# A kernel's opening stage: scratch laid out by half, fewer and larger reloads, the second input's loads and two sums moved

## The chip, the cores and the metric

The kernel runs on one core of one Trainium2 chip. The figure of merit is the device time of one execution in microseconds (us), the median over several runs. A core has five engines that run their own instruction streams and wait for each other through semaphores: TensorE (PE, matrix products; PEld is its loading of weights), VectorE (DVE), ScalarE (ACT), GpSimd (POOL) and SyncE (SP, which here only issues DMAs). ACT and POOL issue DMAs too.

## The reference, cut to what matters

```python
X = np.fft.rfft(x, axis=1)                     # x: 8 x 3008 x 256, float32
Y = X * (filt_r + 1j * filt_i)[None]           # 1505 frequencies x 256 channels
y = np.fft.irfft(Y, n=3008, axis=1).astype(np.float32)
h = y.reshape(24064, 256) @ w_in               # 256 x 2048
g = h * (1.0 / (1.0 + np.exp(-h)))             # SiLU
out = (g @ w_out).astype(np.float32)           # 2048 x 256
```

The two weight matrices arrive as 64-bit floats, the rest as 32-bit floats.

## The kernel before

**The main loop.** The length 3008 is 47 x 64, and each transform is done as matrix products with small tables. The two large products use a scheme with seven block products in place of eight (names A11, A12, S1 to S4, A22), on 2 x 2 blocks of the weights. Work is cut into 384 *steps*: 8 batches, 2 halves of a batch, 3 column ranges, 8 slices `jp` of the hidden width. A step is seven products into the hidden layer (`hidden`, L734, with the SiLU and sums on ACT and DVE) and, one step later, seven out of it (`project`, L797). Step s uses slice s mod 8, so slices 2 and 3 of the weights are first needed in steps 2 and 3. What else there is to do (the spectral stages of the next batch, weights not yet unpacked) is put into the steps as pieces with a step number and a round of eight (`put`), so that it runs beside them.

**The ramp.** Before step 0 batch 0 has to pass through the spectral stages alone, and the weights of the first slices have to be unpacked. This change lies in the ramp's end and in the first two steps. The ramp is written out by hand from L997 to L1111; each engine takes its instructions in that order. Its stages for batch 0 are:

- `stage1_first` (L299): the 47-point part, from x loaded into the room that the weights `w_t` will take later; DVE transposes it into a view `t2`, also within `w_t`.
- For each of six groups g: `forward` (L446), `multiply` by the filter (DVE, L468), `inverse_first` (L511), then `rows_first` (L518, L521), which copies two PSUM banks to SBUF and stores them to a DRAM scratch `d2`. Group g's two stores fill rows 8g to 8g+7 of `d2`.
- `load_t4` (L546) reads `d2` back with other axes on the partitions: rows 0 to 47 of one half h on 48 partitions, four values of n for a piece. It is called for four pieces and three row ranges (0 to 24, 24 to 32, 32 to 48), each time for both halves: 24 DMAs, all on SP but the second half's last four, which are on ACT.
- `stage3` (L562) for pieces 0 to 3, the last 47-point products, and the copies of their results into `y` (L576, or L244 and L246 by turns on DVE and ACT). Step 0 needs all four.

In `d2[row, n, half, channel]` both halves of a row lie side by side for each n, so one half's run of contiguous bytes is 256 channels, 1 KB.

**Fillers.** While PE has nothing to do it multiplies tables into a spare bank (`idle`, 128 columns, L1009; `idle_wide`, 256 columns, L1015; and the `fill` of `stage3`, L554). They compute nothing that is used.

**Weights in the ramp.** `split` (L922, L925 on DVE; L924, L926 and, for some slices, L931, L932 on ACT), `rounded` (L938, L940, L944 on DVE) and `placed` (L953) turn the 64-bit words of slice j into 32-bit floats in `w_t`. `combine_weights(jp)` (L705) forms four sums of 128 x 256 for a pair of slices: pairs 1, 2 and 3 on GpSimd, pair 0 on DVE.

**Batch 1.** `second` is batch 1's part. Its `stage1` (L333, two products of 512 columns, and L349, two copies on ACT) sits in steps 0 to 7; `load_x(0)` and `weights(9)` are issued on SP in the middle of the ramp (L1081, L1082).

**Banks.** In the ramp `bank` hands out the eight PSUM banks in turn by the counter `early`; after the ramp batch 1's stage 1 uses the two banks of tag `f`.

## Time and profile before

| | |
|---|---|
| median of 3 runs | 2583.8 us (2583.6 to 2589.22) |
| the profiled execution, its own time | 2582.95 us |
| its span, first to last instruction | 2581.1 us |
| mean granted TensorE clock | 0.998 |
| PE busy in the span | 2560.4 us (99%) |
| DVE, ACT, POOL busy | 1679.8, 1112.5, 424.0 us |
| the ramp: start of step 0's first product | 80.25 us from the span's start |

The times of lines are microseconds from the start of the span. "Busy" of PE is modelled, since matmuls are pipelined, so 99% busy doesn't say that PE is at its peak; it includes the fillers. One product in the program is two records of PE in the trace: "x42" under L1015 are 21 products. A row of the timeline gives start, length, engine, line, operation, result and operands, count, and in brackets how long the engine was idle before it and what ended that.

### The profile page before, as it was taken

The numbers are of one execution on the slowest core, as the hardware profiler recorded it, in microseconds if no ns is written. First come the engines' busy times: TensorE is split into PE (matmuls) and PEld (weight loads), VectorE is DVE, ScalarE is ACT, GpSimd is POOL, SyncE is SP. The second block draws the span as 40 slices with busy tenths as digits, with TensorE's granted clock in tenths as the row PEclk, the third lists the DMA queues.
The fourth block names the chain that finished last, engine by engine and source line by source line (L and its number), as shares of the span: only waits on it lengthen the run. The fifth ranks groups of instructions, "written<-read, shape, count | busy, mean of one in ns | idle before, by whom it ended". The sixth has DMA issues, their size and how long they took to land.

```text
span 2581.1 us, 48332 instructions
## 1 busy us (share of the span) xinstructions
PE 2560.4 (99%) x18956; PEld 2197.1 (85%) x18956; DVE 1679.8 (65%) x3569; ACT 1112.5 (43%) x3014; POOL 424.0 (16%) x672
## 2 busy tenths in 40 slices
PE   8999999999999999999999999999999999999998
PEld 6788888888888888888888888888888888888987
DVE  7866666666666666666666666666666666555554
ACT  3544444444444444444444444444444444444443
POOL 2211111121112111311122111211121112101101
PEclk9999999999999999999999999999999999999999
DMA  8531232222222222322223122331232211200000
GB/s 279 156 74 49 72 79 63 60 63 75 60 63 69 70 62 58 77 72 66 61 65 83 50 66 58 80 80 46 66 85 64 69 42 33 58 19 16 9 17 17
DMA packets 200077, 171.08 MB, mean 66 GB/s; under 512 B 122116, under 2 KB 174196, under 8 KB 199060
## 3 DMA queue, kind: packets, MB, share of 16 engines
q1 hardware_dynamic: 178520, 117.04, 18.5%
q0 software_dynamic: 16928, 44.65, 5.4%
q10 hardware_dynamic: 4400, 6.29, 0.8%
q8 instruction: 149, 2.44, 0.4%
q14 instruction: 80, 0.66, 0.1%
HBM read 96.05 MB, written 81.26 MB: 69 GB/s over the span
## 4 chain that ended last, share of the span: by engine, by line
PE 96%; DVE 1%; DMA 1%; ACT 1%; issue 0%; ACTq 0%; POOL 0%; SPq 0%; DVEq 0%; POOLq 0%
PE acc L797 43%; PE px L734 25%; PE pyz L734 19%; PE pd L562 3%; PE pb L446 2%; PE pc L489 2%; PE pf L416 1%; DMA filt<-in_filt_r_dram 1%; DVE g L705 0%; DMA w_t<-in_x_dram 0%; PE pa L342 0%; PE pc L511 0%; PE idle L1015 0%; ACT t L349 0%; ACTq L233 0%
## 5 line engine op out<-in xcount | busy, mean ns | idle before, releaser
L797 PE MATMUL acc<-g,w_t 128*128 128x256 f32 (+1 forms) x5376 | 1509.1, 375 | 0.4 <-DVE g L705 0.4
L797 PEld LDWEIGHTS acc<-g,w_t 128*128 128x128 f32 x5376 | 1021.8, 190 | 115.2 <-DVE g L705 0.8
L705 DVE TENSOR_TENSOR g<-pyz,abc 128x256 f32<-128x256 f32 (+1 forms) x1152 | 479.3, 416 | 613.4 <-ACT abc L755 359.6
L705 DVE TENSOR_TENSOR g<-g 128x256 f32<-128x256 f32 (+3 forms) x1152 | 598.2, 519 | 196.5 <-ACT g L738 183.4
L734 PE MATMUL px<-ty,w_t 128*128 128x256 f32 (+1 forms) x2304 | 677.9, 376 | 0.7 <-ACT abc L755 0.6
L738 ACT ACTIVATE g<-g 128x256 f32<-128x256 f32 (+1 forms) x1152 | 472.9, 410 | 250.0 <-DVE g L705 250.0
L734 PEld LDWEIGHTS px<-ty,w_t 128*128 128x128 f32 x2304 | 432.3, 190 | 64.4 <-issue 7.9
L705 POOL TENSOR_TENSOR s<-s 128x256 f32<-128x256 f32 (+1 forms) x329 | 254.7, 791 | 1412.9 <-DVE s L817 1307.8
L734 PE MATMUL pyz<-y,w_t 128*128 128x256 f32 (+1 forms) x1536 | 453.8, 377 | 0.0
L734 PEld LDWEIGHTS pyz<-y,w_t 128*128 128x128 f32 x1536 | 283.2, 189 | 48.1 <-DVE g L705 8.9
L749 ACT COPY abc<-px 128x256 f32<-128x256 f32 (+1 forms) x384 | 141.1, 368 | 365.2 <-PE px L734 365.2
L755 ACT COPY abc<-px 128x256 f32<-128x256 f32 (+1 forms) x384 | 141.6, 369 | 336.3 <-PE px L734 335.6
L738 ACT ACTIVATE g<-px 128x256 f32<-128x256 f32 (+1 forms) x384 | 145.8, 380 | 297.6 <-PE px L734 297.5
L734 PE MATMUL px<-y,w_t 128*128 128x256 f32 (+1 forms) x768 | 231.9, 384 | 0.1
L734 PE MATMUL pyz<-ty,w_t 128*128 128x256 f32 (+1 forms) x768 | 225.3, 375 | 0.2 <-DVE g L705 0.2
L734 PEld LDWEIGHTS px<-y,w_t 128*128 128x128 f32 x768 | 140.0, 189 | 33.2 <-DVE y L584 5.8
L734 PEld LDWEIGHTS pyz<-ty,w_t 128*128 128x128 f32 x768 | 144.3, 190 | 18.8 <-DVE g L705 1.0
L742 ACT COPY abc<-px 128x256 f32<-128x256 f32 (+1 forms) x384 | 135.4, 353 | 43.7 <-PE px L734 43.7
L562 PEld LDWEIGHTS pd<-wi_t,t 48*64 48x64 f32 x4096 | 65.7, 135 | 28.8 <-ACT g L738 16.4
L428 POOL DMA_DIRECT2D d<-tf x144 | 71.4, 503 | 29.5 <-DVE tf L424 25.4
L817 ACT COPY s<-acc 128x512 f32<-128x512 f32 (+1 forms) x94 | 54.2, 577 | 47.6 <-PE acc L797 47.5
L562 PE MATMUL pd<-wi_t,t 48*64 48x47 f32 x4096 | 72.2, 233 | 2.5 <-issue 2.2
(124 smaller groups left out, 1316.0 us busy)
## 6 DMA issues: line engine op xcount, KB each, us to landing
t<-d SPq DMA_DIRECT2D x120, 192.0 KB
d<-q POOLq DMA_DIRECT2D x86, 256.0 KB, 2.6
t<-d SPq DMA_DIRECT2D x84, 256.0 KB
out_dram<-o SPq DMA_DIRECT2D x636, 32.0 KB
d<-tf POOLq DMA_DIRECT2D x144, 96.0 KB, 3.2
xr<-in_x_dram SPq DMA_DIRECT2D x6, 1472.0 KB
x_all<-in_x_dram SPq DMA_DIRECT2D x72, 96.0 KB
x_all<-xr SPq DMA_DIRECT2D x72, 96.0 KB
```

The costliest lines, as they stand in the source:

```text
L428: nc.gpsimd.dma_start(out=d1[k // 2, :, k % 2, n0:n0 + 4], in_=us["tf"][32 * k:32 * k + NS].rearrange("p q n c -> p (q n) c"))
L446: nc.tensor.matmul(out=ps[k][32 * j:32 * j + 32, ri, :], lhsT=d_t[rows, 4 * g + at, ri, :], rhs=t2[rows, at, :], start=True, stop=True)
L489: nc.tensor.matmul(out=ps[j][64 * k:64 * k + 64, a, :], lhsT=e_t[rows, g + a, k, ri, :], rhs=zs[k][rows, ri, :], start=(a == 0 and ri == 0 ...
L562: nc.tensor.matmul(out=ps[h][c0:c0 + 64, cb, i, :], lhsT=t4s[g][rows, i, 128 * cb + c0:128 * cb + c0 + 64], rhs=wi_t[rows, :], start=True, ...
L705: eng.tensor_tensor(out=out, in0=in0, in1=in1, op=op)
L734: nc.tensor.matmul(out=out, lhsT=w_t[:, jp, c, 0], rhs=rhs, start=start, stop=True, skip_group_check=True)
L738: nc.scalar.activation(out=g[:, k, 0:n], in_=g[:, k, 0:n] if src is None else src, func=AFT.Silu)
L742: nc.scalar.copy(out=sums[:, 0, 0:n], in_=xo)
L749: nc.scalar.copy(out=sums[:, 1, 0:n], in_=xo)
L755: nc.scalar.copy(out=sums[:, 2, 0:n], in_=xo)
L797: nc.tensor.matmul(out=acc[pair][i][:, h, 0:n], lhsT=w_t[:, jp, c, 1], rhs=g[:, k, 0:n], start=(jp == 0 and h == 0), stop=last, skip_group ...
L817: copy(out=s[:, 2 * i:2 * i + 2, 0:n], in_=acc[pair][i][:, :, 0:n])
```

## The change

It touches the ramp from group 3 on, and three things in the first steps.

- The scratch of batch 0 becomes `d2[half, row, n, channel]`. The reload of the first 16 n is one row range and one half per DMA (`load_t4_rows`): 6 DMAs, all on SP, each moving 16 KB contiguous per row, in place of 24 with 1 KB pieces. They land in a view `t4` within `w_t` (the room of `t2`, slots that `forward` of groups 2 to 5 reads) instead of four tiles of two pools. The stores write 1 KB pieces instead of 2 KB.
- The first reload (rows 0 to 24) is issued after `forward(5)`; rows 24 to 32 come after group 4's stores in program order, rows 32 to 48 after group 5's.
- Batch 1's `load_x(0)` and `weights(9)` are issued behind all six reloads.
- Group 4's stores go out from ACT instead of GpSimd. Group 5 copies into tiles of pool `z`, its second copy on DVE instead of ACT, and its copies stand behind `rounded(4, 5)`.
- `combine_weights(2)` leaves GpSimd and the ramp; its halves run on DVE at the ends of steps 0 and 1. `combine_weights(3)` stays on GpSimd behind a one-column copy (`gate`) that waits for `placed(8)`.
- Slice 4's last exponent operation goes from two ACT instructions (L931, L932) to one DVE instruction (L940).
- Fillers: 12 wide and 12 narrow products in place of 21 wide ones; the two wide fills in `stage3` of pieces 1 and 2 go. After pieces 1 and 2 batch 1's first two stage 1 products are done (`rows_product`); they leave step 0.
- Copies into `y`: pieces 0 and 1 all on ACT, pieces 2 and 3 one on ACT and one on DVE (before, by turns).
- The bank counter is set so that `stage3` leaves the two `f` banks to `rows_product`.

```diff
-        d2 = dpool.tile([2 * NS, 32, 2, C], FP32, name=f"d2_{b}", tag="d2")
+        d2 = dpool.tile([2 * NS, 32, 2, C] if b else [2, 2 * NS, 32, C], FP32, name=f"d2_{b}", tag="d2")
...
+            us["t4"] = view[:, 8960:13056].rearrange("p (n c) -> p n c", c=C)
...
+        def rows_product(u, h, ps=None):
+            if ps is None:
+                ps = bank(b, f"pa_{b}_{u}_{h}")
+                us.setdefault("rows", []).append(ps)
+            nc.tensor.matmul(out=ps.rearrange("p n c -> p (n c)"), lhsT=wx_t,
+                             rhs=xs[u][0:96, 512 * h:512 * h + 512], start=True, stop=True)
...
         def rows_first(g):
             for i, pool, tag in ((0, qpool, "q"), (1, opool, "o")):
+                if g == NG - 1:
+                    pool, tag = zpool, "z"
                 qt = pool.tile([128, 2, C], FP32, name=f"q_{b}_{g}_{i}", tag=tag)
-                nc.scalar.copy(out=qt, in_=halves[g][i])
+                copy = nc.vector.tensor_copy if g == NG - 1 and i == 1 else nc.scalar.copy
+                copy(out=qt, in_=halves[g][i])
                 a0 = 8 * g + 4 * i
-                queue = nc.gpsimd if g == NG - 2 else nc.scalar
-                queue.dma_start(out=d2[a0:a0 + 4].rearrange("a n h c -> (a n) h c"), in_=qt)
+                nc.scalar.dma_start(out=d2[:, a0:a0 + 4].rearrange("h a n c -> (a n) h c"), in_=qt)
...
+        def load_t4_rows(first, last):
+            for h in range(2):
+                nc.sync.dma_start(out=us["t4"][64 * h + first:64 * h + last], in_=d2[h, first:last, 0:16, :])
...
-                if g == 0:
-                    nc.scalar.copy(out=dst[:, :, h, n0:n0 + 4], in_=ps[h])
-                else:
-                    evac(dst[:, :, h, n0:n0 + 4], ps[h])
+                copy = nc.vector.tensor_copy if g > 1 and h == 1 else nc.scalar.copy
+                copy(out=dst[:, :, h, n0:n0 + 4], in_=ps[h])
...
-            if j in (0, 2, 4, 6):
+            if j in (0, 2, 6):
...
             part["rows_first"](2)
-            for later in range(4):
-                part["load_t4"](later, 0, 24)
-            second["load_x"](0)
-            weights(9)
+        if g == 3:
+            part["load_t4_rows"](0, 24)
...
     part["rows_first"](3)
-    for later in range(4):
-        part["load_t4"](later, 24, 32)
     split(4, 5)
     combine_weights(0)
-    for g in (4, 5):
-        part["rows_first"](g)
+    part["rows_first"](4)
+    part["load_t4_rows"](24, 32)
     rounded(4, 5)
+    part["rows_first"](5)
+    part["load_t4_rows"](32, 2 * NS)
+    second["load_x"](0)
+    weights(9)
     placed(4, 5)
     split(6, 7, 8)
-    combine_weights(2, eng=gp)
-    for g in range(4):
-        part["load_t4"](g, 32, 2 * NS)
     rounded(6, 7)
     placed(6, 7)
-    combine_weights(3, eng=gp)
     rounded(8)
     placed(8)
-    idle_wide(21)
+    gp.tensor_copy(out=gate, in_=w_t[:, 4, A11, 0, 0:1])
+    combine_weights(3, eng=gp)
+    stand = bank(0, "stand")
+    idle_wide(12, stand)
+    idle(12, stand)
     last_x = x_t[1].rearrange("p a n -> p (a n)")[0:96, 0:256]
     for g in range(4):
-        part["stage3"](g, fill=((), (wide_rows,), (wide_rows,), (last_x,))[g])
+        early[0] = 1 if g in (0, 3) else early[0]
+        part["stage3"](g, fill=(last_x,) if g == 3 else ())
+        if g in (1, 2):
+            second["rows_product"](0, g - 1)
     idle_wide(2)
...
+    for k in range(2):
+        put(k, 7, combine_weights, 2, k)
```

More of the change, by code (lines that the diff above doesn't have):

```diff
@@ L221 @@
     warm = cpool.tile([128, 1], FP32)
+    gate = cpool.tile([128, 1], FP32)
     bias_t = cpool.tile([128, 5], FP32)
@@ L236, in load_filters @@
                                     ap=[[94 * C, 16], [t * C, last - first], [1, C]]))
-    flip, early = [0], [0]
-    def evac(dst, src):
-        flip[0] ^= 1
-        if flip[0]:
-            nc.vector.tensor_copy(out=dst, in_=src)
-        else:
-            nc.scalar.copy(out=dst, in_=src)
+    early = [0]
     y = {}
@@ L325, in sums @@
             us[u] = ut
+        def rows_product(u, h, ps=None):
[4 more added lines that the diff above has]
+                             rhs=xs[u][0:96, 512 * h:512 * h + 512], start=True, stop=True)
         def stage1(u):
             t1 = tpool.tile([128, 2, 2, C], FP32, name=f"t1_{b}_{u}", tag="t")
-            ps = [bank(b, f"pa_{b}_{u}_{h}", HIDDEN[h] if b > 1 and u == 6 else None) for h in range(2)]
+            ps = None
+            if b > 1 or u > 0:
+                ps = [bank(b, f"pa_{b}_{u}_{h}", HIDDEN[h] if b > 1 and u == 6 else None) for h in range(2)]
             if b == 1:
-                xt = xs.pop(u)
-                for h in range(2):
-                    nc.tensor.matmul(out=ps[h].rearrange("p n c -> p (n c)"), lhsT=wx_t,
-                                     rhs=xt[0:96, 512 * h:512 * h + 512], start=True, stop=True)
+                if u > 0:
+                    for h in range(2):
+                        rows_product(u, h, ps[h])
+                else:
+                    ps = us["rows"]
+                xs.pop(u)
                 if u + 2 < 8:
@@ L537, in rows, with load_t4 @@
                 nc.gpsimd.dma_start(out=d2[a0:a0 + 4].rearrange("a n h c -> (a n) h c"), in_=qt[:, a])
-        def load_t4(g, first=0, last=2 * NS):
-            if first == 0 and b == 0 and g in (2, 3):
-                t4s[g] = tpool.tile([128, 4, C], FP32, name=f"t4_{b}_{g}", tag="t")
-            elif first == 0:
-                t4s[g] = t4pool.tile([128, 4, C], FP32, name=f"t4_{b}_{g}", tag="t4")
-            for h in range(2):
-                queue = nc.scalar if first == 32 and h == 1 else nc.sync
-                queue.dma_start(out=t4s[g][64 * h + first:64 * h + last],
-                                in_=d2[first:last, 4 * g:4 * g + 4, h, :])
+        def load_t4(g):
+            t4s[g] = t4pool.tile([128, 4, C], FP32, name=f"t4_{b}_{g}", tag="t4")
+            for h in range(2):
+                rows = d2[:, 4 * g:4 * g + 4, h, :] if b else d2[h, :, 4 * g:4 * g + 4, :]
+                nc.sync.dma_start(out=t4s[g][64 * h:64 * h + 2 * NS], in_=rows)
+        def load_t4_rows(first, last):
+            for h in range(2):
+                nc.sync.dma_start(out=us["t4"][64 * h + first:64 * h + last], in_=d2[h, first:last, 0:16, :])
         def stage3(g, home=None, fill=()):
@@ L556, in stage3 @@
                   .rearrange("p (a i n) -> p a i n", a=2, i=4) for t in room]
+            t4 = us["t4"][:, 4 * g:4 * g + 4] if b == 0 and g < 4 else t4s[g]
             for cb in range(2):
@@ L563, in stage3 @@
                                 out=ps[h][c0:c0 + 64, cb, i, :],
-                                lhsT=t4s[g][rows, i, 128 * cb + c0:128 * cb + c0 + 64],
+                                lhsT=t4[rows, i, 128 * cb + c0:128 * cb + c0 + 64],
                                 rhs=wi_t[rows, :], start=True, stop=True)
@@ L574, in stage3 @@
             for h in range(2):
-                if g == 0:
-                    nc.scalar.copy(out=dst[:, :, h, n0:n0 + 4], in_=ps[h])
-                else:
-                    evac(dst[:, :, h, n0:n0 + 4], ps[h])
+                copy = nc.vector.tensor_copy if g > 1 and h == 1 else nc.scalar.copy
+                copy(out=dst[:, :, h, n0:n0 + 4], in_=ps[h])
         def evict_y(g, h):
@@ L584, in evict_y @@
             copy(out=dst[:, :, h, n0:n0 + 4], in_=us["pd", g][h])
-        return dict(evict_y=evict_y, evict_t1=evict_t1, halves=halves, load_first=load_first, stage1_first=stage1_first, load_x=load_x, sums=sums, stage1=stage1, reverse_x=reverse_x,
+        return dict(evict_y=evict_y, evict_t1=evict_t1, halves=halves, load_first=load_first, stage1_first=stage1_first, load_x=load_x, rows_product=rows_product, sums=sums, stage1=stage1, reverse_x=reverse_x,
                     load_fold=load_fold, fold=fold, stage1_fold=stage1_fold, evict_fold=evict_fold,
-                    load_t2=load_t2, forward=forward, multiply=multiply, add=add, inverse=inverse, inverse_first=inverse_first, rows_first=rows_first, even=even, rows=rows, load_t4=load_t4, stage3=stage3)
+                    load_t2=load_t2, forward=forward, multiply=multiply, add=add, inverse=inverse, inverse_first=inverse_first, rows_first=rows_first, even=even, rows=rows, load_t4=load_t4, load_t4_rows=load_t4_rows, stage3=stage3)
     pending = []
@@ L938, in round_weights @@
             v.scalar_tensor_tensor(out=mf, in0=lo, scalar=2.0 ** -52, in1=mf, op0=ALU.mult, op1=ALU.add)
-            if j not in (0, 2, 4, 6):
+            if j not in (0, 2, 6):
                 v.tensor_scalar(out=e, in0=ef, scalar1=255.0, scalar2=float(1 << 23),
```

## The prediction

> **What bounds the kernel now.** I read the page first:

> ```profile
> span 2581.1 us, 48332 instructions
> PE 2560.4 (99%) x18956; PEld 2197.1 (85%) x18956; DVE 1679.8 (65%) x3569; ACT 1112.5 (43%) x3014; POOL 424.0 (16%) x672
> PE 96%; DVE 1%; DMA 1%; ACT 1%; issue 0%; ACTq 0%; POOL 0%; SPq 0%; DVEq 0%; POOLq 0%
> ```

> The whole is bound by PE; 2450 us of it, from about 130 us on, is not touched. So the change can move the time only by when PE leaves the ramp and how it gets through the first steps. For that I read the chain that ended last, up to 140 us (start, length, what):

> ```profile
> 51.67 10.52 PE pc L511 x192
> 62.19 9.26 PE idle L1015 x42
> 71.70 1.21 issue
> 72.90 1.14 PE pd L562 x62
> ...
> 79.35 0.82 ACT y L246
> ...
> 95.93 0.33 DVE g L705
> 96.53 0.76 DVE g L705 x2
> ...
> 128.92 0.35 DVE g L705
> 129.31 0.70 PE pyz L734 x2
> ```

> Two readings. First, between the inverse products (over at 62.19) and `stage3` PE does 9.26 us of fillers, then stands 1.21 us, although the fillers are over: the data of `stage3` is late, at 72.9. Second, from step 0 to 129 us the chain runs through DVE and ACT, not PE: there a step takes about 7.85 us (DVE e of L922 in the chain at 97.66, 105.51, 113.47, 121.32), while PE's 14 products of 0.43 and two of 0.86 make 7.74. PE is all but full, yet DVE sets the pace.

> Why the data is late shows in the timeline, engine by engine (rows of SP, ACT, POOL, then DVE):

> ```profile
> 57.67 0.72 SPq L906 DMA_DIRECT2D raw<-in_moe_w_out_dram  x1
> 62.95 6.58 SPq L546 DMA_DIRECT2D t<-d  x12
> ...
> 62.84 0.33 ACTq L521 DMA_DIRECT2D d<-q  x1
> 63.88 0.33 ACTq L521 DMA_DIRECT2D d<-q  x1
> 69.44 1.88 ACTq L546 DMA_DIRECT2D t<-d  x4
> ...
> 63.62 3.45 POOL L705 TENSOR_TENSOR w_t<-w_t 128x256 f32<-128x256 f32 x4 [0.47 <-DVE w_t L953]
> ...
> 63.45 0.42 DVE L922 TENSOR_SCALAR scratch<-raw 128x512 uint32<-128x512 uint32 x1
> 63.79 0.95 DVE L925 TENSOR_SCALAR scratch<-raw 128x512 uint32<-128x512 uint32 x1
> 88.53 0.42 DVE L705 TENSOR_TENSOR g<-pyz,abc 128x256 f32<-128x256 f32 x1
> ```

> SP waits from 58.4 to 62.95 for group 3's stores, which were issued at 55.94 and 56.93 and by the trace's completion records land at 61.1 and 62.9, among the loads of x and slice 9; then it needs 6.58 us for 12 issues. The last store (63.88) lands at 67.7. The last four reloads stand on ACT behind `split(6, 7, 8)`, to 69.44; the first of them lands at 72.8, which is when `stage3` starts. `split` itself runs slow, 0.95 for 0.42 us, while GpSimd does its four sums.

> [...] the completion of an 8-row reload moves once some 0.1 us after its issue and then eight times as data lands, that of a 16-row reload sixteen times as data lands. [...] PE idle 3.06 us to 32.48, mean clock 0.91 from 20 to 40 us; the 1.21 us stand costs nothing (1.00).

> **The change, part by part.** All times are before's.

> *The reloads.* Group 4 and 5: products end at 62.19. ACT needs no L931 and L932 for slice 4 (0.71 and 0.72), so group 4's copies and stores go at 59.7 to 61.2. Group 5's first copy is 0.58 and its issue 0.33: 62.2 to 63.15. Its second is on DVE, behind `rounded(4, 5)`: without ACT's L931 and L932, but with one more L940 (0.42), this still ends at 62.07, so the copy runs 62.25 to 62.95 (a 128x512 DVE operation from PSUM is 0.68) and ACT issues its store at 63.2 to 63.5. Landing: 2.5 us from issue (the store at 50.52 lands at 53.0), so 65.7. SP then issues two reloads, 0.43 each. The 16-row reload of 67.83 landed 2.2 us after its issue with 4 KB for each engine; now it is 16 KB, for which the trace's nearest packet (12 KB in 0.46) gives 0.61. First half 68.4, second 69. Rows 0 to 24 go at 53.1 on 12 engines, two rows of 0.61 each and half, done by 58; rows 24 to 32 wait for group 3's stores, which now have no loads of x and weights among them (59.5). Both are hidden. So data is there at **69.0**, against 72.8.

> *The fillers.* 12 wide at 9.26/21 = 0.441 are 5.29. A narrow one: eight at L1009 from 47.78 to 49.76, 0.2475 each, 12 are 2.97. PE reaches `stage3` at 62.19 + 8.26 = **70.45**; this, not the data, is now last, with 1.4 us to spare. Against 72.90: −2.45.

> *Within `stage3`.* Before, 6.29 us (72.90 to 79.19): four pieces and three fills of 0.63 (73.97 to 74.60). After: two fills less, −1.26; two products of 512 columns, 0.86 and the same 0.19 for changing over, +2.10. +0.84. x for them is issued at 66.6, behind the reloads, and needs some 3.6 us: there by 70.2, wanted at 72.7; hidden. ACT has six copies of 0.75 to 0.86 from 71.6 on and PE is longer, so no bank is late. Then 1.06 to step 0 as before (the last copy). Step 0's start: 80.25 − 2.45 + 0.84 = **78.64**, −1.61.

> *Step 0.* The two products it loses were 1.72 of PE; but the chain there is y, ty, g, e (DVE), e, m (ACT), and the two copies L349. None moves. PE waits instead: 0. If PE were the limit it would be −1.7.

> *The sums of pair 2.* Off GpSimd: DVE's `split` gets back about 4 x 0.53 = 2.1, which is hidden (`placed(8)` ends about 73.8 instead of 76.5; step 0 is later). On DVE: a dependent pair 0.34 + 0.43 = 0.77 at step 0's end (as 109.46 in the chain) and an independent one, 0.67, at step 1's. Queued behind each are g's next sum, then `split(10)` or `split(11)`, then ACT. DVE's slack there is 0.12 before 88.53 (its previous operation ends at 88.41) and none at 96.53. So +0.65 + 0.67 = **+1.32**, and since the chain stays with DVE to 129, it isn't won back. Bounds: 0 if PE, which is nearly as full, would have made DVE wait anyway; 1.44 with no slack.

> *Nothing else.* The gated sums of pair 3 run on GpSimd from 73.8, 2.9 to 3.9 us, and are wanted in step 3; DVE's copies of y read PSUM. Nothing on SP is behind anything later than before. Piece 4 and 5's reloads get 4 KB runs; hidden.

> Sum: −2.45 + 0.84 + 1.32 = **−0.3 us** on the profiled 2582.95 (span 2581.1 and 1.85 around it). The median of the runs is 0.85 above that execution: 2583.8 − 0.3 = **2583.5**.

> **The rivals.**
> - *The sums on DVE are hidden.* For: PE's records in steps 1 to 6 leave no gap of theirs, so DVE's lead may be a tie. Against: the chain. −1.6: 2582.2.
> - *Slower: the reloads are late.* One mechanism: stores and reloads in series behind group 5, with all of `stage3` behind one wait in place of four pieces that each waited for its own. For: before needed 9 us from store to use. Against: 1.4 us to spare. Decides from 70.45 on, each us costs one; at 73 it is +2.3 (2586). PE would be cold after about 3 us of standing, +1.7. To leave 0.3% the data would have to come at about 77.
> - *PE goes cold in step 0.* Without the two products its PE has about 2.6 us of gaps, but in pieces of 0.3 to 1.2, shorter than the stand at 71.70 that cost nothing. If it did: up to +1.7 for 3.4 us at half clock, 2585.
> - *The shifted work isn't on the path at all*, so that step 0 starts as before: then only +1.3, 2585.

> **How the numbers follow.** Forecast 0.42, sums hidden 0.25, late reloads 0.13, cold PE or no gain 0.12, and something that I haven't seen 0.08. 0.3% is 7.75 us, about what a measurement of this kernel can tell from no change; none of the named cases reaches it, so same takes all but a late reload gone far wrong or the unseen: 0.90 same, 0.06 slower, 0.04 faster. The range takes in the hidden sums with shorter fillers (−2.7, 2581) and late reloads (2587), and a us for the spread of the runs.

> **What would show it.** Right: fillers from 62.2 to 70.4 with no stand after them; 6 reloads on SP, the last issued near 66; step 0 at 78.6; the DVE operations after 86 offset by −1.6, after 96 by −0.3; PE from 130 us on the same. Wrong: an "issue" piece before L570 in the chain (late data), a clock under 1.00 between 70 and 90, or step 0 at 80 or later.

## The result, and the profile after

The changed kernel takes 2595.71 us in the median of four runs (2593.55 to 2596.37), against 2583.95 us (2583.6 to 2589.22) for the kernel before on the same chip. The ratio is 1.0039, with a 95% interval of 1.0022 to 1.0057; here and below ratios are worked out from the single executions, so they aren't the quotient of the medians (1.0046). It is slower by some 12 us, where a gain of 0.3 was forecast, and outside the predicted range of 2580 to 2588. The ratio lies beyond the 0.3% (7.75 us) that was taken as the bound, but its interval reaches below that. The profiled execution took 2595.21 us, its span is 2593.4 us, and the mean granted clock of TensorE is 0.995 (0.993 to 0.995 in the four executions) where before had 0.998.

From the page of the kernel after, the span, the busy times and the shares of the chain that ended last:

```profile
span 2593.4 us, 48308 instructions
PE 2568.1 (99%) x18958; PEld 2201.3 (85%) x18958; DVE 1678.5 (65%) x3574; ACT 1112.4 (43%) x3012; POOL 419.1 (16%) x667
PE 96%; DMA 1%; DVE 1%; ACT 1%; issue 1%; SPq 0%; ACTq 0%; DVEq 0%
```

PE is busy for 7.7 us more with two records more: a count of busy time can't say where the 12 us lie. The chain can. Kernel after, the chain that ended last in order of time (start, length, what):

```profile
51.85 10.52 PE pc L516 x192
62.37 5.38 PE stand L1021 x24
67.75 2.69 PE stand L1015 x24
70.44 3.61 issue
74.33 1.53 issue
75.86 3.66 PE pd L570 x126
79.52 2.00 PE pa L325 x2
...
90.16 0.85 PE px L740 x2
...
141.74 0.70 PE pyz L740 x2
```

The fillers end at 70.44, as forecast. Then PE stands 5.1 us (two pieces of "issue", with two small products at 74.05 between them) before `stage3` can begin in earnest at 75.86. In `stage3` each thing takes 1.6 to 1.9 times as long as at full clock: two pieces, 126 records of L570, 3.66 us, where before took 1.14 for 62; a product of 512 columns, two records, 2.00 (2.08 in the timeline) where e1_fill below has 1.12 in its timeline. Step 0 starts at 89.95 (before 80.25). The last line answers to before's 129.31: +12.43. After that nothing more is added.

Kernel after, a row of the timeline of SP and one of ACT, and from SP's waits between 36 and 92 us the first (us waited, times, longest):

```profile
53.31 16.94 SPq L554 DMA_DIRECT2D w_t<-d  x6
```

```profile
63.02 0.89 ACTq L528 DMA_DIRECT2D d<-q  x2
```

```profile
SPq L554 <- DMA d<-q: 22.3, 6, 7.1
```

Group 5's stores are issued at 63.02 and 63.48, as forecast. But the six reloads spread over 16.94 us, and what SP waits for, before every one of them, is a store. In the trace's completion records the stores of group 5 land at 68.84 and 69.42, not at 65.7; the last two reloads go at 69.48 and 69.85 and land at 73.84 and 75.77.

The third reading is the clock. Kernel after, busy times of each engine in stretches of the ramp's end (columns: the stretch and its length, then PE, PEld, DVE, ACT and POOL with their instructions, granted clock, DMA share, GB/s):

```profile
72.00:76.00 4.00, 0.42 (x8) 0.36 (x11) 2.32 (x5) 0.00 (x0) 1.81 (x4) 0.86 0.75 122
76.00:90.00 14.00, 14.00 (x265) 10.18 (x266) 2.40 (x4) 4.44 (x6) 1.28 (x2) 0.50 0.32 85
```

From 74.86 to 91.93 us, for 17.07 us, TensorE runs at half clock, and again from 95.34 to 98.76 (3.41). All of `stage3` lies in it, with PE busy for 14.00 of 14 us. By the chain some 7.4 us of it are the small products of L570, the rest wider ones.

So the difference up to step 3's first product, at 115.03 against 102.61, splits like this:

| stretch | before, us | after, us | difference |
|---|---|---|---|
| start of `stage3`, from the span's start | 72.90 | 75.86 | +2.96 |
| `stage3` to step 0 | 7.35 | 14.09 | +6.74 |
| step 0 to step 1 | 6.64 | 7.79 | +1.15 |
| step 1 to step 2 | 7.83 | 8.64 | +0.81 |
| step 2 to step 3 | 7.89 | 8.65 | +0.76 |
| sum | | | +12.42 |

The profiled times differ by 2595.21 − 2582.95 = 12.26.

### The profile page after: what moved, and what is told of

Same layout as the page of the kernel before. It is cut to its first block, busy times and chain, and to the rows that moved or that the text cites. A ratio compares the mean times of both kernels' runs of the same rounds, so it can differ in the third digit from the quotient of the medians.

```text
span 2593.4 us, 48308 instructions
## 1 busy us (share of the span) xinstructions
PE 2568.1 (99%) x18958; PEld 2201.3 (85%) x18958; DVE 1678.5 (65%) x3574; ACT 1112.4 (43%) x3012; POOL 419.1 (16%) x667
## 4 chain that ended last, share of the span: by engine, by line
PE 96%; DMA 1%; DVE 1%; ACT 1%; issue 1%; SPq 0%; ACTq 0%; DVEq 0%
PE acc L803 43%; PE px L740 25%; PE pyz L740 19%; PE pd L570 3%; PE pb L451 2%; PE pc L494 2%; PE pf L421 1%; DVE g L711 0%; DMA w_t<-in_x_dram 0%; PE pa L347 0%; PE pc L516 0%; PE pa L325 0%; DMA filt<-in_filt_i_dram 0%; ACT t L354 0%; DMA e_t<-e_tbl 0%
## 5 line engine op out<-in xcount | busy, mean ns | idle before, releaser
L740 PEld LDWEIGHTS px<-ty,w_t 128*128 128x128 f32 x2304 | 432.2, 190 | 66.6 <-issue 7.4
L570 PEld LDWEIGHTS pd<-wi_t,t 48*64 48x64 f32 x3840 | 61.3, 135 | 25.9 <-ACT g L744 16.4
L853 DVE STREAM_TRANSPOSE o<-s 128x256 f32<-128x256 f32 x192 | 73.9, 423 | 0.7 <-issue 0.3
```

The lines of the kernel that those rows point to most:

```text
L570: nc.tensor.matmul(out=ps[h][c0:c0 + 64, cb, i, :], lhsT=t4[rows, i, 128 * cb + c0:128 * cb + c0 + 64], rhs=wi_t[rows, :], start=True, sto ...
L740: nc.tensor.matmul(out=out, lhsT=w_t[:, jp, c, 0], rhs=rhs, start=start, stop=True, skip_group_check=True)
L853: v.transpose(out=o[:, :, h, :], in_=results[pair][:, ((2, 6), (4, 1))[chunk][h], :])
```

## The experiments

The theory after this reading: (1) the six large reloads are slow and hold up the stores behind them, so `stage3`'s data comes 6.8 us later than forecast; (2) the 5 us of standing halve the clock, and `stage3`'s small products don't bring it back; (3) the sums of pair 2 on VectorE cost 0.65 to 0.8 each. Rivals: that the loss in `stage3` is not the clock but something in the changed order; that the late data comes from the order of the queues alone and not from the 16 KB pieces; that the longer steps 1 and 2 are an after-effect of the clock and not the sums. Each experiment below but the probes and the last one starts from the kernel after or goes on from another; medians and ratios are against the kernel before, timed on the same chip beside them (2582.96 us for the first four, 2583.46 for the last three).

### The stand filled with work: e1_fill

```diff
-    idle_wide(12, stand)
+    idle_wide(25, stand)
```

> The changed kernel with 25 wide fillers in place of 12 (5.7 us more), so that PE doesn't stand before the last reload lands (75.8 us in the changed kernel's trace). If the half clock is what makes the lateness expensive: reloads land at the same 75.8, stage3 runs its pieces in about 1.1 us instead of 1.9, step 0 starts near 84.2 instead of 89.95, no clock under 1.00 after 40 us, and the median is near 2589 (5 us over before: 3.9 late at step 0, 1.3 for the sums on DVE). If the late data alone costs 12 us, whatever the clock does: step 0 again near 90 and the median near 2595.

Measured: 2591.65 us (2588.73 to 2593.12), ratio 1.003 [1.0021, 1.0039], 8.7 us over before in the medians, where the kernel after was 11.8 over; the profiled execution 2592.33. Its timeline of PE:

```profile
76.36 2.02 PE L570 MATMUL pd<-wi_t,w_t 48*64 48x47 f32 x117
79.11 0.43 PE L570 MATMUL pd<-wi_t,w_t 48*64 48x47 f32 x11 [0.72 <-issue]
79.47 1.12 PE L325 MATMUL pa<-x_all,wx_t 96*128 96x512 f32 x2
...
85.27 0.67 PE L740 MATMUL px<-y,w_t 128*128 128x256 f32 x2
```

The data is as late as before (`stage3` at 76.36), but two pieces now take 2.45 us and a product of 512 columns 1.12. `stage3` to step 0 is 8.91 instead of 14.09, although there is a stand before the last 11 records of the second piece, for which no wait shows (it is taken up at m2_bare). So the half clock in `stage3` comes of the stand ahead of it, and not of the changed order. But the clock is not safe with that: the trace has it at half from 89.53 to 96.36, in step 0, which takes 7.25 us in place of 6.64, and step 1 takes 9.69. Step 0 without the two products of 512 columns has gaps, here of 1.16 and 0.72 us. They don't decide by themselves: e4_gap below has the same step 0, with gaps of 1.16 and 0.85 us, and kept the full clock.

### The reloads piece by piece again: e2_pieces

```diff
-            for h in range(2):
-                nc.sync.dma_start(out=us["t4"][64 * h + first:64 * h + last], in_=d2[h, first:last, 0:16, :])
+            for g in range(4):
+                for h in range(2):
+                    nc.sync.dma_start(out=us["t4"][64 * h + first:64 * h + last, 4 * g:4 * g + 4],
+                                      in_=d2[h, first:last, 4 * g:4 * g + 4, :])
```

> The changed kernel with each row range reloaded by piece of four n: 24 DMAs with 4 KB contiguous, piece by piece, both halves in turn, all on SP. If the 16 KB packets hold up the stores on the DMA engines that they share: group 5's stores land before 67.5 instead of at 69.4, and piece 0 of the last range lands before 71, so stage3 starts at 70.5 to 71.5, the clock stays at 1.00, step 0 starts near 79 and the median is within 2 us of before. If the stores are late because they now write 1 KB pieces, or because the layout as such is slow to read: they land near 69 again and stage3 starts after 73.

Measured: 2591.04 us (2588.76 to 2593.5), ratio 1.0029 [1.0017, 1.004]. The same bytes go to the same partitions, in 24 DMAs of 4 KB pieces. Group 5's stores are issued at 63.26 and 63.72 and land at 65.89 and 67.0; the first piece's last reloads land at 69.25 and 69.68, and `stage3` starts without a stand. Its timeline of PE:

```profile
70.02 2.18 PE L572 MATMUL pd<-wi_t,w_t 48*64 48x47 f32 x128
74.75 1.72 PE L325 MATMUL pa<-x_all,wx_t 96*128 96x512 f32 x2 [2.56 <-DMA x_all<-in_x_dram]
...
84.90 1.06 PE L742 MATMUL px<-y,w_t 128*128 128x256 f32 x2
```

So it is the size of the pieces, and that one DMA carries what all four parts of `stage3` need, that made the data late: 70.02 against 75.86. The two were changed together, and this run doesn't weigh them against each other. The early data was forecast rightly; the full clock and a median within 2 us of before were not. But PE now stands 2.56 us in the middle of `stage3`, for batch 1's x: issued behind the reloads at 70.64, it lands at 74.62, and the products that were moved forward wait for it. The clock falls at 75.09 for 13.7 us, and step 0 starts at 84.90. In the kernel after this wait is covered by the first: x lands at 77.03, and the products come at 79.52.

### Without the early reloads: e3_skip

```diff
-        if g == 3:
-            part["load_t4_rows"](0, 24)
...
-    part["load_t4_rows"](24, 32)
```

> The changed kernel without the reloads of rows 0 to 24 and 24 to 32: stage3 multiplies what lay there before, so this part of batch 0's spectral result is left out; the work on PE is the same. If the early reloads hold up the stores: group 5's stores land 2.5 us after issue (near 66 instead of 69.4) and the last two reloads, issued near 66, land near 72.3, since their own 512 KB still take 6.3 us from issue. If the stores are slow by themselves: 69.4 and 75.8 again. Step 0 near 81 in the first case, with the clock at 1.00 [...].

One execution, 2591.96 us. Nothing now stands before the stores: issued at 62.70 and 63.11, they land at 64.86 and 65.60, 2.2 and 2.5 us after their issue, as the forecast had them. So the early reloads cost the 3.7 us. The last reloads go at 65.75 and 66.14 and land at 70.35 and 72.14, still 6.4 us from the first issue to the second landing. A row of its timeline of PE:

```profile
72.19 3.66 PE L570 MATMUL pd<-wi_t,w_t 48*64 48x47 f32 x126 [1.47 <-DMA w_t<-d]
```

Stands of 0.33 and 1.47 us went with a half clock here, from 71.90 on for 17.1 us, where a full one was forecast. Before stood 1.21 us at 71.70 with no such effect. Ahead of the stand were narrow products in this kernel, wide ones in before; this run alone doesn't say whether that decides.

### The sums in a gap of VectorE: e4_gap

On top of e1_fill, the sums of pair 2 are done between `split` and `rounded` of slices 9 and 10, where VectorE waits for ScalarE:

```diff
-    for k in range(2):
-        put(k, 7, combine_weights, 2, k)
...
-        put(j - 9, 1, lambda j=j: (split(j), rounded(j)))
+        put(j - 9, 1, lambda j=j: (split(j), j < 11 and combine_weights(2, j - 9), rounded(j)))
```

> e1_fill, with the two halves of the sums of pair 2 put on DVE between the split and the rounding of slices 9 and 10 (where DVE waits about 0.97 us for ACT) instead of at the ends of steps 0 and 1. If the sums lay on the path from step 0 to 129 us: the split of slice 10 and of slice 11 come 0.65 and 1.3 us earlier after step 0's start than in e1_fill and the median is 1.3 us under e1_fill's. If PE would have made DVE wait anyway: the same within 0.3 us.

Measured: 2589.13 us (2586.93 to 2598.29), ratio 1.0021 [1.0013, 1.003]; 2.5 less than e1_fill in the medians, where 1.3 was forecast (e1_fill's profiled execution also loses its clock in step 0). Steps 0, 1 and 2 take 6.64, 7.84 and 7.89 us, before's lengths (6.64, 7.83, 7.89), with a full clock throughout. The chain of the kernel after in the last part of step 1's work on VectorE, where the two sums of the weights stand between g's:

```profile
107.67 0.34 DVE g L711
...
108.27 0.76 DVE w_t L711 x2
109.03 0.68 DVE g L711 x2
```

and of e4_gap in the same place, where g's follow each other:

```profile
101.13 0.34 DVE g L711
...
101.74 0.76 DVE g L711 x2
```

The sums were on the path, and a gap was there that takes them for nothing. For their size e2_pieces is the better run: its sums stand where the kernel after has them, its clock is full from 88.74 on, and its steps 1 and 2 take 8.32 and 8.64 us, 0.49 and 0.75 over before. e4_gap's profiled execution, 2588.74, is 5.79 over before, and its step 0 is 5.20 later (85.45): 3.21 of that is the later start of `stage3` (76.11), 0.84 the two products within it, and 1.15 another stand in the second piece:

```profile
79.28 0.43 PE L570 MATMUL pd<-wi_t,w_t 48*64 48x47 f32 x11 [1.15 <-issue]
```

### What a reload costs by itself: e5_probe and e7_probe2

Both put probe DMAs ahead of before's ramp, all with 16 KB rows of x; e5_probe a dozen one after the other with different destination partitions, e7_probe2 ten, each after a VectorE instruction that clears the room, so that none overlaps the next. The core of the second:

```diff
+    def probe_to(p0, rows, queue=nc.sync, first=0, runs=1):
+        dst = probe[p0:p0 + rows, 0:4096].rearrange("p (k n) -> p k n", k=runs)
+        queue.dma_start(out=dst, in_=rows_of(rows, first, runs))
...
+        clear()
+        probe_to(32, 16)
+        clear()
+        probe_to(32, 16, runs=4)
+        clear()
+        probe_to(32, 16)
+        probe_to(96, 16, queue=nc.scalar, first=16)
+        clear()
+        probe_to(32, 16)
+        probe_to(96, 16, first=16)
```

> The kernel before, with a dozen DMAs ahead of everything that nothing uses, one after the other, from rows of x to w_t, 16 KB per row: 16 rows to partitions 32 to 47; 128 rows; 16 again; 64 rows; 8 rows to partitions 24 to 31; 32 rows; 16 rows to partitions 0, 4, ... 60; 16 rows to 0, 8, ... 120; 16 rows to 32 to 47 in 4 KB pieces; then 16 rows to 32 to 47 from SP with 16 to 96 to 111 from ACT at once; then the same two both from SP. Only the DMA packets are looked at. If the destination sets the rate [...]: packets to 32 to 47 take about 2.1 us each for 16 at once [...], to 24 to 31 the same for 8 at once [...], the 4 KB pieces the same total as the 16 KB ones, and SP with ACT together finish both in little more than one alone. If the size of the packet or the row stride in DRAM sets it: the same packet time wherever 16 rows go, and the 4 KB pieces faster in total.

> The kernel before, with ten probe transfers put in front of its ramp, each after VectorE has cleared the room it writes, so that none overlaps the next; two rounds of five. All read rows of x. (a) 16 rows of 16 KB to partitions 32 to 47; (b) the same bytes to the same partitions in pieces of 4 KB; (c) (a), and at the same time 16 rows to partitions 96 to 111 from ACT's queue; (d) as (c), but both issued on SP; (e) 8 rows of 16 KB to partitions 24 to 31. If the neighbouring destination partitions set the rate: (a) some 125 to 150 GB/s, or about 1.9 us for its 256 KB, (b) the same rate, (d) twice the time of (a), and (c) clearly less than (d), if partitions 96 to 111 have ways of their own. If the size of a piece sets it: (b) clearly faster than (a). If the 16 DMA engines themselves set it: (c) takes what (d) takes. (e) 1.6 us or more for 128 KB. The whole some 60 to 90 us longer than before.

From the trace's packets, first start to last end (both rounds of e7 where there are two):

| probe | run | GB/s | median of a 16 KB packet, us |
|---|---|---|---|
| 128 rows to all partitions | e5 | 349 to 352 | 0.61 |
| 64 rows to 0 to 63 | e5 | 187 | 1.28 |
| 32 rows to 0 to 31 | e5 | 183 | 1.11 |
| 16 rows to 0, 4, ... 60 | e5 | 191 | 0.96 |
| 16 rows to 0, 8, ... 120 | e5 | 188 | 0.95 |
| 16 rows to 32 to 47 | e5, e7 | 124 to 150 | 1.2 to 1.4 |
| the same in 4 KB pieces | e7 | 126, 125 | (0.19 for 4 KB) |
| 16 to 32 to 47 and 16 to 96 to 111, both SP | e7 | 124, 132 | 1.81, 1.69 |
| 8 rows to 24 to 31 | e5, e7 | 75; 80, 91 | 0.79; 1.07, 1.33 |

In these probes the destination sets the rate, not the size of a piece: 4 KB pieces to partitions 32 to 47 are no faster (125 and 126 GB/s, against 124 to 150), and sixteen rows spread over 0 to 60 move a quarter to a half faster (191). What it is about the destination that does it, the probes don't show. The packet times expected for e5_probe were too long, 2.1 us where 1.2 to 1.4 (partitions 32 to 47) and 0.79 (24 to 31) were measured; 2.1 us comes with a second reload behind the first. The two halves on one queue take 6.30 and 6.22 us from the first issue to the second landing; in the kernel after it was 6.29. With the second half on ACT's queue it was 6.12 in the first round (6.46 in the second, which has two table loads among it): no gain to speak of. The likely reason is that a reload of 16 rows already has a packet on each of the 16 engines (its completion comes in 16 parts): ACT's first packet starts at 25.03 us, 0.78 after SP's first, though both DMAs were issued at 23.3. Which engine moved a packet isn't in the trace. e5_probe's own comparison of the two queues is inconclusive, since ACT's DMA ran together with another probe; e7_probe2 was made to settle that.

### All mended: m1_fills

Reloads by piece, 18 wide fillers and no narrow ones, fills in `stage3` again and batch 1's two products back in step 0, the sums in VectorE's gaps; group 5's other tiles, its copy on VectorE, the scratch by half and the second input behind the reloads stay. The part not shown above:

```diff
-    idle_wide(12, stand)
-    idle(12, stand)
+    idle_wide(18, stand)
...
-        early[0] = 1 if g in (0, 3) else early[0]
-        part["stage3"](g, fill=(last_x,) if g == 3 else ())
-        if g in (1, 2):
-            second["rows_product"](0, g - 1)
+        part["stage3"](g, fill=((), (wide_rows,), (wide_rows,), (last_x,))[g])
```

> A mended version of the changed kernel: reloads by piece (as in e2_pieces), 18 wide fillers and no narrow ones, stage3's wide fills of pieces 1 and 2 back and batch 1's two products back in step 0, the sums of pair 2 in DVE's waits of steps 0 and 1 (as in e4_gap). If the account of the loss is right (late and lumped reloads, PE at half clock, sums on DVE's path): stage3 starts at 70.2 (e2_pieces had it at 70.0), step 0 at 77.6 against 80.25, steps as long as before's, no clock under 1.00 after 40 us, and the median 2.5 us under before's. If something else of the change costs time: the median not under before's.

Measured: 2580.35 us (2579.45 to 2586.67), ratio 0.9986 [0.9978, 0.9994]: faster than both kernels, by 3 us of before's 2583.46. Its timeline of PE:

```profile
70.81 1.24 PE L567 MATMUL pd<-wi_t,w_t 48*64 48x47 f32 x64
71.97 0.70 PE L558 MATMUL pd<-d_t,wx_t 96*128 96x256 f32 x2
...
78.22 0.67 PE L737 MATMUL px<-y,w_t 128*128 128x256 f32 x2
```

Step 0 starts at 78.22, 2.0 earlier than in the kernel before, 0.4 earlier than was forecast for the kernel after and 0.6 later than was expected of this run; steps 0 to 2 take 6.64, 7.84 and 7.89, and the clock is full. An earlier `stage3` can be had, and it is worth what it moves.

### Without the fills inside `stage3`: m2_bare

```diff
-        part["stage3"](g, fill=((), (wide_rows,), (wide_rows,), (last_x,))[g])
-    idle_wide(2)
+        part["stage3"](g, fill=(last_x,) if g == 3 else ())
+    idle_wide(4)
```

> m1_fills without stage3's two wide fills (0.63 us each) and with 4 in place of 2 fillers after it. If stage3's small products keep PE's clock up by themselves: step 0 about 1 us earlier than in m1_fills, the copies on ACT and DVE being last, and the median a further 1 us down. If they don't count as activity: half clock within stage3 or just behind it, step 0 later than m1_fills' by 2 to 5 us.

Measured: 2582.43 us (2579.35 to 2586.73), ratio 0.9987 [0.998, 0.9994], in the median 2 more than m1_fills, though the two ratios don't tell them apart. In the profiled execution, 2583.46, PE stands within the third piece:

```profile
74.77 0.79 PE L567 MATMUL pd<-wi_t,w_t 48*64 48x47 f32 x39 [1.62 <-issue]
```

The clock is halved from 76.05 to 82.88, and step 0 starts at 81.58, 3.4 later than in m1_fills. The two fills, which compute nothing, are worth that in this execution.

What PE stands for is not the pieces' data: the third piece had landed by 72.17, and the next PE record that waits for anything comes 56 records after the stand. The record points to PE's own instructions. The page lists a DMA queue for them:

```profile
q8 instruction: 149, 2.44, 0.4%
```

Its 149 packets of 16 KB are 64 bytes for each of the 38129 PE records of this trace, weight loads included, so a packet holds about 256 of them. The unexplained stands of e1_fill, e4_gap (the same program up to there) and m2_bare all end at PE's record 1730, though in m2_bare that is in the third piece and in the others in the second, and each follows a packet of this queue: packet over at 77.71, 77.96 and 73.23, PE on at 79.11, 79.28 and 74.76. Where that record comes late enough there is no stand (1.22 us after the packet in the kernel before, 1.50 in m1_fills): with the wide fills PE took 3.36 us for the 256 records before it, in m2_bare 2.08. So the fills may help by making PE use up its instructions more slowly, as well as by what they are to the clock. No experiment was made on this; it is a reading of the traces.

### The second input's move alone: e6_behind

Before, with `load_x(0)` and `weights(9)` behind all reloads and nothing else changed:

```diff
-            second["load_x"](0)
-            weights(9)
...
+    second["load_x"](0)
+    weights(9)
```

> The kernel before with one part of the change alone: batch 1's load_x(0) and weights(9) issued behind all reloads. If the loads of x and slice 9 are what held group 3's stores (landing 61.1 and 62.9): these land by 60, SP issues the reloads of rows 24 to 32 some 2 to 3 us earlier, and stage3 starts at the end of the fillers, 71.5 to 72, instead of 72.9; median down by about 1 us. If the early reloads hold the stores: they land within 1 us of before's and the start stays at 72.9.

Measured: 2588.95 us (2586.43 to 2591.56), ratio 1.0016 [1.001, 1.0023]: slower, by 5.5 us in the medians. Group 3's stores do land 1.3 us earlier (59.83 and 61.62, against 61.1 and 62.9), but the last reloads of the second half, on ACT behind its `split` work, are issued at 69.95 and later (69.44 in before), and x, at 70.18 on SP, now goes in among them; the last three of them land at 75.28, 75.73 and 76.04 (73.46, 73.78 and 74.21 in before). Its timeline of PE:

```profile
72.94 1.14 PE L562 MATMUL pd<-wi_t,t 48*64 48x47 f32 x62 [0.73 <-DMA t<-d]
...
75.42 1.67 PE L562 MATMUL pd<-wi_t,t 48*64 48x47 f32 x62 [0.47 <-DMA t<-d]
```

Two stands of 0.73 and 0.47 us with small products and one wide fill between them, and the clock is at half from 75.80 to 89.45; before, with one stand of 1.2 us behind wide fillers, kept it. So this edit by itself doesn't pay.

## Why the prediction was wrong

**"The reloads": the step that failed.** Data at 69.0 was forecast, 75.8 was measured. 3.7 us of it are the stores of group 5: issued when forecast, landing at 69.42 instead of 65.7. The forecast called the early reloads "both hidden", because nothing waits for them. But half of each store waited behind them. Rows 24 to 32 went out at 61.44 and 61.75, and each of the two reloads has eight completions behind a first one, as if on eight engines (before's reloads of 24 rows have twelve: at 54.91 to 55.45 for the one issued at 53.09). The trace doesn't number the engines, but it fits eight that the two reloads and the stores have in common: of the 16 completions of group 4's second store, issued at 61.56, eight come at about 63.8 and eight between 67.5 and 68.7. Of the 16 KB packets in the way the first eight took 2.0 to 2.7 us each, the second eight 0.9 to 1.3. e3_skip, without them, has 2.2 to 2.5 us for the stores; e2_pieces, with 4 KB packets, 2.6 to 3.3. The forecast counted the engines of such a reload; that they would be in the stores' way was not drawn from it.

The other 3.0 us are the last reloads: 6.29 from the first issue to the second landing, 3.3 forecast. The packet price of 0.61 was taken from 12 KB packets of a transfer to many partitions. It is right for that (0.61 with 128 rows), and wrong for 16 neighbouring ones: 0.8 to 1.8 for the first half and 2.14 to 2.15 for all of the second. Before's last reloads, 64 KB each to their 16 partitions, move at no better a rate (the four on ACT's queue 256 KB in 2.4 us, some 107 GB/s), but its piece 0 needs two of them, and after's needs all 512 KB.

**The rival "Slower: the reloads are late" named the mechanism,** with one wait for all of `stage3`, and where it decides, 70.45. It had a chance of 0.13 and too small a price. By its own rule, 75.86 − 70.45 = 5.41 us of lateness give 2582.65 + 5.4 + 1.7 for a cold clock = 2589.8. Measured were 7.05 for the clock instead of 1.7: 6.74 − 0.84 in `stage3` and 1.15 in step 0. With that, 2582.95 − 0.3 + 5.41 + 7.05 = 2595.1, against 2595.21. The 1.7 was half of 3.4 us at half clock, as long as before's trace has it (3.41 us, from 32.59 on, after the stand of 3.06); in the kernel after it was 17.07 and 3.41 us. From 78.28 to 88.52 PE is never idle in the profile; 5.16 of these 10.24 us are `stage3`'s products of 48 x 64 with 47 columns, the rest wider ones, and the clock doesn't come back. From 88.52 to 91.93 there are none of the small ones, and after that the clock is full. The data "at about 77" that would leave 0.3% was therefore asked for too late: 75.8 did it.

**"PE goes cold in step 0"** was a rival with up to +1.7, held off by the shortness of its gaps. In the kernel after step 0 is half cold from the start (+1.15); in e1_fill, which enters it with a full clock, it goes cold there by itself (half clock from 89.53 to 96.36). e4_gap, with the same step 0, and m1_fills, with the two products back, do not. The term of 0 for step 0 holds for its chain (6.64 us in e4_gap, as before) and not always for the clock.

**"x … hidden" was wrong,** though it decided nothing in the kernel after: in e2_pieces, where the data comes at 70, the products wait 2.56 us for x. Forecast was x there at 70.2; behind the reloads it was issued at 70.64.

**What held.** "The fillers": 62.37 to 70.44, 70.45 forecast. "Within `stage3`": +0.84 forecast at full clock; e4_gap takes 9.34 − 1.15 for its unexplained stand = 8.19 from the start of `stage3` to step 0, against 7.35, which is +0.84. "The sums of pair 2": +0.65 and +0.67 forecast, +0.81 and +0.76 in the two steps after step 0. e4_gap, where both go, shows that they come with the sums; since the clock is at half to 98.76, within step 1, and e2_pieces has +0.49 and +0.75 at full clock, a part of the +0.81 may be the clock. "Nothing else": steps from 3 on are as before, and `split` runs at 0.42 us with GpSimd idle beside it, as forecast.

**How firm the clock is.** Before's own times have two groups: of the 83 executions timed beside the experiments, 61 took at most 2586 us at a mean granted clock of 0.997 to 0.999, and 18 took over 2588, at 0.995 or 0.996. Half clock for 14 to 17 us is worth that difference in the mean clock (17.1 us x 0.5 / 2581 = 0.003), so before itself seems to lose its clock in about one execution of five; no profile of such an execution was taken, and this rests on the clocks alone. m1_fills shows it in 1 of 15 (2586.67, 0.995). Whether a stand of about 1 us before products of this size costs the clock isn't settled by these runs: after 1.21 us it was full in before's profiled execution, with stands of 0.33 and 1.47 us it was halved in e3_skip's, and "the 1.21 us stand costs nothing" was read from one execution.

Open: whether PE's stands within `stage3` in e1_fill, e4_gap and m2_bare are waits for instructions, as the traces suggest; what kind of work keeps or brings back the full clock; and whether narrow fillers ahead of a stand make the clock fall sooner (e3_skip), which was not tried apart.

## What to carry to other kernels

A transfer that nobody waits for isn't hidden for that reason alone: here two reloads of 8 rows made the stores behind them, which somebody waits for, land 5.8 to 5.9 us after their issue instead of 2.2 to 2.5. Count what a transfer's packets put ahead of the next store, and price a packet from a transfer to as few and as neighbouring partitions (here 1.2 us and more in the median), not from one to all 128 (0.61). Merging loads also merges their waits, so the first consumer waits for the last byte (here `stage3` began at 75.86, and at 70.02 with reloads by piece). And a stand of one or two microseconds at the edge of a stage of small matrix products is priced with the clock that it may cost (17.1 us at half clock from 71.90 on in e3_skip, with stands of 0.33 and 1.47 us): two wide fills that compute nothing, put between the small products, were worth 2 us in the medians here and 3.4 at step 0 in the profiled executions.
